# A diffusion transformer block on one core: where the attention gate's vectors are made and stored, which token tile fc1 begins with, the order of the MLP weight blocks, and TensorE's semaphore

## The chip, the cores and the metric

The kernel runs on one core of one Trainium2 chip. The metric is device time in microseconds (us) of one execution, as the median of several runs. A core has a matrix engine (TensorE, PE in the profile; PEld is its weight load), VectorE (DVE), ScalarE (ACT), GpSimd (POOL) and SyncE (SP), which here only issues DMAs. The engines run their own instruction streams in order and wait for one another through semaphores.

## The reference

One block of a diffusion transformer on 2 images of 256 tokens of width 1152, two heads of 576, an MLP of 4608. A conditioning vector per image gives six modulation vectors of 1152: shift, scale and gate for attention and for the MLP.

```python
mod = (_silu(c) @ w_mod).reshape(B, 6, 1, D)
shift_a, scale_a, gate_a, shift_m, scale_m, gate_m = [mod[:, i] for i in range(6)]
h = _layernorm(x) * (1 + scale_a) + shift_a
q, k, v = split(h @ wqkv)
attn = _softmax(einsum('bqhd,bkhd->bhqk', q, k) * Dh ** -0.5)
a = einsum('bhqk,bkhd->bqhd', attn, v) @ wo
x = x + gate_a * a
h2 = _layernorm(x) * (1 + scale_m) + shift_m
m = _gelu(h2 @ w_fc1) @ w_fc2
return x + gate_m * m
```

## The kernel before, in words

**The planner.** The kernel is written as a list of units (an operation, or a group of matmuls) on five engines. `schedule` plays the list through with costs and puts each engine's units in an order; TensorE's and SP's orders are those of the program text, the others' follow priority, and `S.in_order` fixes chosen sequences by hand. `emit` then writes the instructions, with a wait wherever one reads or overwrites what another engine made. Each instruction that is no DMA raises its engine's semaphore by one; a DMA raises one of 66 semaphores by 16 when it has landed.

**The memory.** All tiles are views of one SBUF arena, so a region serves several things in turn. Four slots hold blocks of fc1's weight, `WFC1[q % 4]`: block q, 1152 KB, has the columns of hidden tiles f = 4q to 4q+3. `WFC2` lies where `WMODR` and `WGM` (parts of the modulation weight) and, at its end, the normalized rows `XN2` lay before; it is loaded in four blocks of 2592 KB, `wfc2_load(0)` to `(3)`.

**Up to the attention.** Layer norm, the scale and shift of attention, K, then Q, the scores and softmax per image b and head h (`s_and_softmax`, index 2b+h), V (`v_proj`), then P times V (`pv`), and between its heads the matmuls of the MLP's shift and scale rows (`rows`). The softmax result is turned on VectorE (`PT_turn`) and moved by four DMAs on SP's queue.

**The attention gate** (`attn_gate`, L1059). gate_a for both images is made on VectorE, hidden under the matmuls: for each of 9 slices of the weight, kt, and each image, 1152 columns are multiplied by the image's scalar and accumulated (L1064, L1067; 18 operations). Then per image a transpose and a sum (L1073, L1075), three small copies, three adds, a cast and a transpose for both images at once (L1079 to L1085). `gate_store` puts the result into scratch memory in HBM by two DMAs, and a load per image spreads it over all 128 partitions (`GA[b]`). All four of these DMAs are on SP's queue, ahead of `wfc1_load(0)` and `(1)`.

**The output projection** (`wo_tile(t)`, t = 0 to 3, 128 tokens each; tiles 0 and 1 are image 0). Three pieces of 384 columns of 9 matmuls each; VectorE multiplies a piece by the gate as it takes it from PSUM (L1171), GpSimd adds x (L1172), VectorE makes the statistics (L751, L752, L754), GpSimd the reciprocal root (L755) and the bias (L1176, L1177), ScalarE the normalized rows `xn2_t` (L1178). Tile 1 is transposed on TensorE (`xn2_T(1)`, L1189) and modulated from PSUM (L1194 on VectorE for kt 0 to 3, L1197 on ScalarE for the rest). Tiles 0, 2 and 3 are turned on VectorE (`xn2_turn`, h2turn, L1204), moved by four DMAs each on SP's queue (`xn2_move`, L1209) and modulated in place (L1214 ScalarE, L1217 VectorE).

**fc1** (`fc1_tile(f, tok0, ntok)`): 9 matmuls into one PSUM bank, one gelu on ScalarE (L1227). The bank comes from a list `acc` that the output projection and fc2 use too. Before: f = 0 to 2 in pieces of 128 tokens, tile 0 first, then tile 1; f = 3 to 13 for image 0; f = 0 to 13 (below `F0`) for image 1, then f = 14 to 35 for all 512 tokens. The MLP's gate (`mlp_gate`, from `WGM`) is made on VectorE meanwhile; its stores and loads are on GpSimd's queue.

**fc2**: 12 output pieces of 36 matmuls in the order of j = 0 to 35, so the first block of `WFC2` (`wfc2_load(0)`), loaded last, is read first. VectorE multiplies by the gate (L1315), adds x (L1316), SP stores.

Every DMA is issued in one helper (L684), every matmul in one (L703), every transpose on TensorE in another (L706), most copies from PSUM in L698 (ScalarE) and L700 (VectorE).

Of the kernel before, what the change touches and what calls it, by code (L numbers as in the profile page):

```python
# [171 lines left out]
class Sched:  # L172
# [233 lines left out]
    def emit(self, nc, block, sems, dma_sems):  # L406
# [6 lines left out]
        dj = 0  # L413
        for e in ENGINES:
            for u in order[e]:
                for ins in u.instrs:
                    if u.dma_bytes > 0:
                        if e == "sp":
                            k = di % n_sp
                            di += 1  # L420
                        else:
                            k = n_sp + dj % n_other
                            dj += 1
                        dma_cnt[k] += 16
                        ins.dma_sem = k
                        ins.dma_val = dma_cnt[k]
                    else:
                        eidx[e] += 1
                        ins.eidx = eidx[e]
# [13 lines left out]
        for u in allu:  # L443
            e = u.eng
            kn = known[e]
            for ins in u.instrs:
                need = {}
                for d in ins.deps:
                    k, v = sem_of(d)
# [52 lines left out]
ALU = mybir.AluOpType  # L502
# [14 lines left out]
F0 = 14  # L517
# [34 lines left out]
def build_kernel(nc, x, c, wqkv, wo, w_mod, w_fc1, w_fc2, out):  # L552
# [5 lines left out]
    with (  # L558
# [75 lines left out]
        GBA = sb(O_R + FG * 17, 192)[0:32, :]  # L634
        GTA = sb(O_R + FG * 17 + 192, 192)[0:32, :]
# [423 lines left out]
        def attn_gate():  # L1059
# [10 lines left out]
            pool(100, lambda e: e.memset(GBA, 0.0), [], [GBA], "gba0")  # L1070
            for b in range(2):
                a_, t_ = ACCA[:, b, :], ACTA[:, b, :]
                dve(150 + FG * 1.1, lambda e, a_=a_, t_=t_: e.transpose(t_, a_), [a_], [t_], "ga_T%d" % b)  # L1073
                t3, o = t_.rearrange("p (g r) -> p g r", r=32), GPA[:, 0, b, :]
                dve(150 + FG * 1.1, lambda e, t3=t3, o=o: e.tensor_reduce(out=o, in_=t3, axis=AX.X, op=ALU.add), [t3], [o], "ga_red%d" % b)  # L1075
            gp = GPA.rearrange("p q b g -> p q (b g)")
            for q in range(1, 4):
                i_, o_ = gp[32 * q:32 * q + 32, 0, :], gp[0:32, q, :]
                dve(200, lambda e, i_=i_, o_=o_: e.tensor_copy(o_, i_), [i_], [o_], "ga_mv%d" % q)  # L1079
            for a_, b_ in ((0, 1), (2, 3), (0, 2)):  # L1080
                x_, y_ = gp[0:32, a_, :], gp[0:32, b_, :]
                dve(200, lambda e, x_=x_, y_=y_: e.tensor_tensor(out=x_, in0=x_, in1=y_, op=ALU.add), [x_, y_], [x_], "ga_add%d" % b_)
            g0, gb = gp[0:32, 0, :], GBA[:, 0:8 * NG]
            dve(200, lambda e: e.tensor_copy(gb, g0), [g0], [gb], "ga_bf")
            last_red[0] = dve(200, lambda e: e.transpose(GTA, GBA), [GBA], [GTA], "ga_t")  # L1085

        def gate_store():
            lin = scratch[0].rearrange("b (g c) -> (b g) c", c=32)
            dma(lin[0:64].rearrange("(j p) c -> p j c", j=2), GTA[:, 0:64].rearrange("p (j c) -> p j c", j=2), 4096, "st_ga0")
            dma(lin[64:72], GTA[0:8, 64:96], 512, "st_ga1")  # L1090

# [59 lines left out]
        acc = [3, 4, 5, 2]  # L1151
# [123 lines left out]
        wo_tile(3, {2: lambda: xn2_T(1)})  # L1275
# [26 lines left out]
        for t in range(4):  # L1302
# [4 lines left out]
            for (c0, c1) in pieces:  # L1307
# [3 lines left out]
                for j in range(JT):  # L1311
# [8 lines left out]
        ga = ["ga_%d_%d" % (b, kt) for kt in range(KT) for b in range(2)]  # L1320
        S.in_order("dve", ga)
        S.in_order("dve", ga[9:10] + ["smax_0", "snb_0"] + ga[10:11] + ["sri_0"] + ga[11:12] + ["smax_2", "snb_2", "PT_turn0", "smax_1", "snb_1", "sri_2"]
                   + ga[12:13] + ["smax_3", "snb_3", "sri_1", "PT_turn2"] + ga[13:14] + ["PT_turn1", "sri_3"] + ga[14:15] + ["PT_turn3"] + ga[15:16])
        S.in_order("act", ["sexp_0_0", "sexp_0_1", "qk_ev8", "spn_0_0", "spn_0_1", "v_ev0_0", "sexp_2_0", "sexp_2_1", "sexp_1_0", "sexp_1_1", "v_ev0_1",
                           "spn_2_0", "spn_2_1", "spn_1_0", "spn_1_1", "v_ev0_2", "sexp_3_0", "sexp_3_1", "v_ev1_0", "spn_3_0", "spn_3_1", "v_ev1_1", "v_ev1_2"])
        S.in_order("dve", ["ga_t", "mt_0", "mt_1", "OT_ev0_7", "OT_ev1_7"])
# [4 lines left out]
                           "bn_ln2_1_0", "wo_t1_1_2", "bn_ln2_1_1", "h2turn_0", "wo_t1_2_0", "bn_ln2_1_2", "aggr_ln2_1", "veps_ln2_1", "wo_t1_2_1", "bn_ln2_2_0", "wo_t1_2_2", "bn_ln2_2_1", "wo_t1_3_0", "bn_ln2_2_2", "aggr_ln2_2", "veps_ln2_2", "h2T_0_0", "h2T_0_3", "h2T_0_6", "wo_t1_3_1",  # L1331
                           "h2T_1_0", "h2T_1_1", "h2T_1_2", "h2T_1_3", "bn_ln2_3_0", "wo_t1_3_2", "bn_ln2_3_1", "h2turn_2", "bn_ln2_3_2", "aggr_ln2_3", "veps_ln2_3"])
        S.in_order("act", ["xn2_0", "xn2_1", "h2T_0_1", "h2T_0_2", "h2T_0_4", "h2T_0_5", "h2T_0_7", "h2T_0_8", "h2T_1_4", "h2T_1_5", "h2T_1_6", "h2T_1_7", "h2T_1_8", "gelu_0_0", "xn2_2"])
# [53 lines left out]
```

## Time and profile before

| | us |
|---|---|
| median of 3 runs | 242.55 (242.41 to 242.78) |
| the profiled execution | 244.14 |
| its span, first to last instruction | 242.4 |
| TensorE busy in the span | 235.8 (97%) |
| VectorE / ScalarE / GpSimd busy | 121.4 / 73.2 / 20.5 |
| mean granted TensorE clock | 0.993 of full |

A row of the timeline has the start in us, the duration in us (of a merged group: to its last end), the engine, the line, the operation, output and input, the count, and in brackets the engine's idle time before it with what ended it. In the chain of waits each piece is a start, a duration and what ran. A row of a wait names the work that came last by the profile's record. In the views of DMAs the last number is the time from issue to landing. Matmuls overlap in their pipeline and their ends are modelled, so that a busy TensorE may still be waiting a little; the pace of the operations that follow it tells more. A row of a view by windows has the stretch and its length, the busy time and count of each engine, the granted clock, the DMA engines' busy share and GB/s.

### The profile page before, as it was taken

How to read it: one execution, taken by the hardware profiler on the slowest of the kernel's cores; microseconds unless marked ns; L12 is line 12 of the kernel's file. 1: busy time of each engine (PE TensorE's matmuls, PEld its weight loads, DVE VectorE, ACT ScalarE, POOL GpSimd, SP SyncE). 2: the span in 40 equal slices, each digit the busy share in tenths (PEclk: the TensorE clock that was granted, in tenths of full speed). 3: DMA queues.
4: the chain of work that ended last, by engine and by line, in shares of the span. 5: the costliest groups of instructions: out<-in, count | busy, mean ns of one | idle time of the engine just before them, and what ended most of it. 6: DMA issues, size and time to landing. Idle time of an engine off the chain costs nothing.

```text
span 242.4 us, 4085 instructions
## 1 busy us (share of the span) xinstructions
PE 235.8 (97%) x1728; PEld 147.6 (61%) x1728; DVE 121.4 (50%) x222; ACT 73.2 (30%) x155; POOL 20.5 (8%) x42
## 2 busy tenths in 40 slices
PE   6899999999999999999998999999999999999995
PEld 2588844456567666887883444444656665665664
DVE  2644469979994598742199997000022222111112
ACT  4922440447635425875332322222000000000000
POOL 1300000000000278310000001200000000000000
PEclk9979999999999999999999999999999999999999
DMA  6999999999590875927999999991000000000000
GB/s 213 366 376 391 389 392 391 395 410 386 168 362 3 230 258 135 308 62 257 388 383 355 388 350 388 368 391 40 0 16 19 16 16 19 16 16 19 20 27 18
DMA packets 34428, 53.00 MB, mean 219 GB/s; under 512 B 4075, under 2 KB 19819, under 8 KB 34411
## 3 DMA queue, kind: packets, MB, share of 16 engines
q1 hardware_dynamic: 34016, 52.14, 61.8%
q0 software_dynamic: 224, 0.59, 0.7%
q8 instruction: 13, 0.21, 0.4%
q10 hardware_dynamic: 171, 0.01, 0.0%
q14 instruction: 4, 0.03, 0.0%
HBM read 50.15 MB, written 1.19 MB: 212 GB/s over the span
## 4 chain that ended last, share of the span: by engine, by line
PE 90%; DVE 3%; DMA 3%; POOL 1%; SPq 1%; issue 1%; ACT 0%; DVEq 0%
PE psum L703 89%; DMA arena<-in_w_mod_dram 3%; DVE arena L1171 1%; SPq L684 1%; DVE arena L751 1%; POOL arena L1172 1%; PE psum L706 0%; DVE arena L1194 0%; DVE arena L1217 0%; ACT arena L1227 0%; POOL arena L755 0%; DVE arena L1315 0%; DVE arena L752 0%; DVE arena L1316 0%; POOL arena L1176 0%
## 5 line engine op out<-in xcount | busy, mean ns | idle before, releaser
L703 PE MATMUL psum<-arena 128*128 128x384 bf16 (+8 forms) x1682 | 233.9, 308 | 3.6 <-POOL arena L729 1.5
L703 PEld LDWEIGHTS psum<-arena 128*128 128x128 bf16 (+1 forms) x1682 | 144.7, 97 | 90.6 <-issue 3.3
L1315 DVE TENSOR_TENSOR arena<-psum,arena 128x384 f32<-128x384 f32 (+2 forms) x13 | 6.9, 528 | 76.1 <-PE psum L703 76.1
L1227 ACT ACTIVATE arena<-psum 128x256 bf16<-128x256 f32 (+2 forms) x53 | 24.0, 460 | 42.2 <-PE psum L703 42.1
L698 ACT ACTIVATE arena<-psum 128x512 bf16<-128x512 f32 (+5 forms) x35 | 18.6, 561 | 31.0 <-PE psum L703 31.0
L1067 DVE SCALAR_TENSOR_TENSOR arena<-arena 128x1152 f32<-128x1152 bf16 x16 | 22.1, 1406 | 0.0
L1100 DVE SCALAR_TENSOR_TENSOR arena<-arena 128x1152 f32<-128x1152 bf16 x16 | 21.3, 1410 | 0.0
L1172 POOL TENSOR_TENSOR arena<-arena 128x384 f32<-128x384 f32 x12 | 10.9, 912 | 71.1 <-DVE arena L1171 71.0
L751 DVE BATCH_NORM_STATS2 arena<-arena 128x6 f32<-128x384 f32 (+1 forms) x18 | 9.7, 551 | 5.6 <-DMA arena<-in_x_dram 4.4
L1178 ACT ACTIVATE arena<-arena 128x1152 bf16<-128x1152 f32 x4 | 5.4, 1348 | 10.2 <-POOL arena L1177 10.2
L1171 DVE TENSOR_TENSOR arena<-psum,arena 128x384 f32<-128x384 f32 x12 | 6.5, 547 | 2.5 <-PE psum L703 2.4
L700 DVE CAST arena<-psum 128x512 bf16<-128x512 f32 x8 | 5.4, 690 | 3.5 <-PE psum L703 3.4
L1316 DVE TENSOR_TENSOR arena<-arena 128x384 bf16<-128x384 f32 (+2 forms) x13 | 6.9, 527 | 0.5
L1204 DVE STREAM_TRANSPOSE arena<-arena 128x1152 bf16<-128x1152 bf16 x3 | 4.1, 1379 | 3.6 <-ACT arena L1178 3.6
L1214 ACT ACTIVATE arena<-arena 128x128 bf16<-128x128 bf16 x12 | 5.0, 482 | 1.0 <-DMA arena<-arena 0.9
L1097 DVE TENSOR_SCALAR arena<-arena 128x1152 f32<-128x1152 bf16 x2 | 1.5, 816 | 7.5 <-DMA arena<-in_w_mod_dram 7.5
L684 POOL DMA_DIRECT2D dit_scratch<-arena x2 | 1.4, 677 | 46.2 <-DVE arena L1115 46.2
L1217 DVE TENSOR_SCALAR arena<-arena 128x128 bf16<-128x128 bf16 x15 | 3.6, 310 | 3.0 <-DMA arena<-arena 3.0
L1018 ACT ACTIVATE arena<-psum,arena 128x256 bf16<-128x256 f32 x8 | 3.7, 469 | 2.4 <-DVE arena L1015 1.9
L706 PEld LDWEIGHTS psum<-arena 128*128 128x128 bf16 (+1 forms) x46 | 3.1, 101 | 1.6 <-DMA arena<-in_c_dram 1.3
L706 PE MATMUL psum<-arena 128*128 128x128 bf16 (+1 forms) x46 | 3.6, 222 | 0.4 <-DMA arena<-in_c_dram 0.4
L755 POOL TENSOR_TENSOR arena<-arena 128x1 f32<-128x1 f32 x6 | 3.4, 564 | 4.3 <-DVE arena L754 4.1
(66 smaller groups left out, 64.6 us busy)
## 6 DMA issues: line engine op xcount, KB each, us to landing
arena<-in_w_fc_dram SPq DMA_DIRECT2D x9, 1152.0 KB, 13.7
arena<-in_w_fc_dram SPq DMA_DIRECT2D x4, 2592.0 KB, 16.8
arena<-in_wqkv_dram SPq DMA_DIRECT2D x18, 288.0 KB, 8.7
arena<-in_w_mod_dram SPq DMA_DIRECT2D x6, 864.0 KB, 12.4
arena<-in_w_mod_dram SPq DMA_DIRECT2D x3, 1728.0 KB, 21.1
arena<-in_wqkv_dram SPq DMA_DIRECT2D x1, 2592.0 KB, 17.9
arena<-in_wo_dram SPq DMA_DIRECT2D x1, 2592.0 KB, 9.6
arena<-in_w_mod_dram SPq DMA_DIRECT2D x1, 2592.0 KB, 10.6
```

The costliest lines, as they stand in the source:

```text
L698: act(c_act(n), lambda e: e.activation(out=dst, in_=src, func=ACTF.Copy), [src], [dst], name)
L700: return dve(c_dve_psum16(n) if psum16 else c_dve_psum32(n), lambda e: e.tensor_copy(dst, src), [src], [dst], name)
L703: S.instr(lambda e: e.matmul(o, lhsT=l, rhs=r, start=st, stop=sp, **kw), reads=[l, r], writes=[o])
L706: S.instr(lambda e: e.transpose(o, i_, idn), reads=[i_, idn], writes=[o])
L751: dve(550, lambda e, s=s, o=o: e.bn_stats(out=o, in_=s), [s], [o], "bn_%s_%d" % (tag, ci))
L1067: ga_units[(b, kt)] = dve(150 + FG * 1.1, lambda e, o=o, w=w, s1=s1: e.scalar_tensor_tensor(out=o, in0=w, scalar=s1, in1=o, op0=ALU.mult, ...
L1100: u = dve(1300, lambda e, o=o, w=w, s1=s1: e.scalar_tensor_tensor(out=o, in0=w, scalar=s1, in1=o, op0=ALU.mult, op1=ALU.add), [w, s1, o], ...
L1171: dve(550, lambda e, o=o, ga=ga, x1c=x1c: e.tensor_tensor(out=x1c, in0=o, in1=ga, op=ALU.mult), [o, ga], [x1c], "wo_t1_%d_%d" % (t, ci))
L1172: S.op("pool", 930, lambda e, xs=xs, x1c=x1c: e.tensor_tensor(out=x1c, in0=x1c, in1=xs, op=ALU.add), reads=[x1c, xs], writes=[x1c], name=" ...
L1227: act(c_act(ntok), lambda e: e.activation(out=dst, in_=o, func=ACTF.Gelu_apprx_tanh), [o], [dst], "gelu_%d_%d" % (f, tok0))
L1315: dve(c_dve_psum32(w), lambda e, o=o, gm=gm, t1=t1: e.tensor_tensor(out=t1, in0=o, in1=gm, op=ALU.mult), [o, gm], [t1], "fc2_t1_%d_%d" % ( ...
L1316: dve(c_dve_32(w), lambda e, t1=t1, x1c=x1c, ost=ost: e.tensor_tensor(out=ost, in0=t1, in1=x1c, op=ALU.add), [t1, x1c], [ost], "fc2_out_%d ...
```

## The change

Five things change together.

1. The attention gate is finished per image. Image 0's accumulations run first (all nine slices, with six of image 1's in front), then its transpose, sum and small operations between softmax steps, then image 1's. Image 0's two stores and its load, and image 1's two stores, go on GpSimd's queue; image 1's load stays on SP's, behind `wfc1_load(0)` and `(1)`.
2. fc1 begins with tile 1: f = 0 to 4 for tokens 128 to 255, then for 0 to 127, then f = 5 to 14 for image 0, f = 0 to 14 for image 1, the rest for all tokens (`F0` is 15). `xn2_T(1)` stands one piece of the output projection earlier, and the hand-made orders of VectorE and ScalarE put tile 1's statistics and pieces ahead of tile 0's turn and pieces.
3. The list of PSUM banks is six long from the output projection on; it was four, and six from image 1's half of fc1 on.
4. `wfc2_load(1)` no longer stands ahead of fc1's blocks 4 and 5: the order on SP's queue after `WGM` is fc1 4, 5, fc2 1, fc1 6, fc2 2, fc1 7, fc2 3, fc1 8, fc2 0. It was fc2 1, fc1 4, 5, fc2 2, fc1 6, 7, fc2 3, fc1 8, fc2 0.
5. TensorE's instructions raise its semaphore only where another engine waits for that instruction.

```diff
@@ emit @@
+        told = {d.gidx for ins in self.instrs for d in ins.deps if d.unit.eng == "pe" and ins.unit.eng != "pe"}
...
                 for ins in u.instrs:
+                    if e == "pe" and ins.gidx not in told:
+                        ins.eidx = None
+                        continue
...
-                    else:
+                    elif ins.eidx is not None:
                         bi.then_inc(sems[e], 1)
@@ build_kernel @@
-F0 = 14
+F0 = 15
...
-        GBA = sb(O_R + FG * 17, 192)[0:32, :]
-        GTA = sb(O_R + FG * 17 + 192, 192)[0:32, :]
+        GBA = [sb(O_R + FG * 17 + b * 256, 128)[0:32, :] for b in range(2)]
+        GTA = [sb(O_R + FG * 17 + b * 256 + 128, 128)[0:32, :] for b in range(2)]
@@ attn_gate @@
             for b in range(2):
-                a_, t_ = ACCA[:, b, :], ACTA[:, b, :]
+                a_, t_, gp = ACCA[:, b, :], ACTA[:, b, :], GPA[:, :, b, :]
                 dve(... e.transpose(t_, a_) ..., "ga_T%d" % b)
                 dve(... e.tensor_reduce(out=o, in_=t3, ...) ..., "ga_red%d" % b)
+                for q in range(1, 4):
+                    dve(200, ... e.tensor_copy(o_, i_) ..., "ga_mv%d_%d" % (b, q))
+                for m_, n_ in ((0, 1), (2, 3), (0, 2)):
+                    dve(200, ... e.tensor_tensor(...) ..., "ga_add%d_%d" % (b, n_))
+                pool(100, ... e.memset(gall, 0.0) ..., "gba0_%d" % b)
+                dve(200, ... e.tensor_copy(gb, g0) ..., "ga_bf%d" % b)
+                last_red[0] = dve(200, ... e.transpose(gt, gall) ..., "ga_t%d" % b)
...
+        def gate_store(b):
+            lin = scratch[0, b].rearrange("(g c) -> g c", c=32)
+            dma(lin[0:32], GTA[b][:, 0:32], 2048, "st_ga%d_0" % b, eng="pool")
+            dma(lin[32:36], GTA[b][0:4, 32:64], 256, "st_ga%d_1" % b, eng="pool")
+        def gate_load(b, eng="sp"):
+            dma(GA[b], scratch[0, b].partition_broadcast(P), P * D * 2, "ld_g%d" % b, eng=eng, run=2304)
...
-        acc = [3, 4, 5, 2]
+        acc = [2, 3, 4, 6, 5, 7]
...
-        gate_store()
-        for b in range(2):
-            dma(GA[b], scratch[0, b].partition_broadcast(P), P * D * 2, "ld_g%d" % b, run=2304)
+        gate_store(0)
+        gate_load(0, "pool")
         wfc1_load(0)
         wfc1_load(1)
+        gate_store(1)
+        gate_load(1)
...
-        wo_tile(3, {2: lambda: xn2_T(1)})
+        wo_tile(3, {1: lambda: xn2_T(1)})
...
-        for tok0 in (0, 128):
-            for f in range(0, 3):
+        for tok0 in (128, 0):
+            for f in range(0, 5):
                 fc1_tile(f, tok0, 128)
-        for f in range(3, F0):
+        for f in range(5, F0):
             fc1_tile(f, 0, 256)
-        wfc2_load(1)
         mlp_gate(last_h2T[0])
-        k = acc_rr[0] % 4
-        acc[:] = [6, 7] + acc[k:] + acc[:k]
-        acc_rr[0] = 0
...
             if f % 4 == 0 and f // 4 >= 4:
-                if f in (24, 32):
-                    wfc2_load((f - 8) // 8)
+                if f >= 24:
+                    wfc2_load(f // 4 - 5)
                 wfc1_load(f // 4)
@@ orders by hand @@
-        S.in_order("dve", ["ga_t", "mt_0", "mt_1", "OT_ev0_7", "OT_ev1_7"])
+        ... ["OT_ev0_7", "mt_0", "mt_1", "OT_ev1_7"] behind "ga_t1"
 VectorE:
-  "bn_ln2_1_1", "h2turn_0", "wo_t1_2_0", "bn_ln2_1_2", "aggr_ln2_1", "veps_ln2_1", "wo_t1_2_1"
+  "bn_ln2_1_1", "wo_t1_2_0", "bn_ln2_1_2", "aggr_ln2_1", "veps_ln2_1", "h2turn_0", "wo_t1_2_1"
...
-  "h2T_0_0", "h2T_0_3", "h2T_0_6", "wo_t1_3_1", "h2T_1_0" ... "h2T_1_3", "bn_ln2_3_0", "wo_t1_3_2", "bn_ln2_3_1", "h2turn_2", "bn_ln2_3_2"
+  "h2T_1_0" ... "h2T_1_3", ..., "wo_t1_3_1", "wo_t1_3_2", "h2T_0_0", "h2T_0_3", "h2T_0_6", "bn_ln2_3_0", "bn_ln2_3_1", "bn_ln2_3_2", ..., "h2turn_2", "h2turn_3"
 ScalarE:
-  "xn2_1", "h2T_0_1" ... "h2T_0_8", "h2T_1_4" ... "h2T_1_8", "gelu_0_0", "xn2_2"
+  "xn2_1", "h2T_1_4" ... "h2T_1_8", "h2T_0_1" ... "h2T_0_8", "gelu_0_128", "xn2_2"
```

More of the change, by code (lines that the diff above doesn't have):

```diff
@@ L413, in emit @@
         dj = 0
+        told = {d.gidx for ins in self.instrs for d in ins.deps if d.unit.eng == "pe" and ins.unit.eng != "pe"}
+        self.told = told
         for e in ENGINES:
@@ L448, in emit @@
                 for d in ins.deps:
+                    if e == "pe" and d.unit.eng == "pe":
+                        continue
                     k, v = sem_of(d)
@@ L1069, in attn_gate @@
                                                 [w, s1, o], [o], "ga_%d_%d" % (b, kt))
[L1070 removed]
             for b in range(2):
[L1072 removed]
+                a_, t_, gp = ACCA[:, b, :], ACTA[:, b, :], GPA[:, :, b, :]
                 dve(150 + FG * 1.1, lambda e, a_=a_, t_=t_: e.transpose(t_, a_), [a_], [t_], "ga_T%d" % b)
[L1074 removed]
+                t3, o = t_.rearrange("p (g r) -> p g r", r=32), gp[:, 0, :]
@@ L1075, in attn_gate @@
                 dve(150 + FG * 1.1, lambda e, t3=t3, o=o: e.tensor_reduce(out=o, in_=t3, axis=AX.X, op=ALU.add), [t3], [o], "ga_red%d" % b)
[L1076 to L1090, printed above, removed]
+                for q in range(1, 4):
+                    i_, o_ = gp[32 * q:32 * q + 32, 0, :], gp[0:32, q, :]
+                    dve(200, lambda e, i_=i_, o_=o_: e.tensor_copy(o_, i_), [i_], [o_], "ga_mv%d_%d" % (b, q))
@@ new lines, in attn_gate @@
+                for m_, n_ in ((0, 1), (2, 3), (0, 2)):
+                    x_, y_ = gp[0:32, m_, :], gp[0:32, n_, :]
+                    dve(200, lambda e, x_=x_, y_=y_: e.tensor_tensor(out=x_, in0=x_, in1=y_, op=ALU.add), [x_, y_], [x_], "ga_add%d_%d" % (b, n_))
+                g0, gall, gb, gt = gp[0:32, 0, :], GBA[b], GBA[b][:, 0:4 * NG], GTA[b]
+                pool(100, lambda e, gall=gall: e.memset(gall, 0.0), [], [gall], "gba0_%d" % b)
+                dve(200, lambda e, gb=gb, g0=g0: e.tensor_copy(gb, g0), [g0], [gb], "ga_bf%d" % b)
@@ new lines, in attn_gate @@
+                last_red[0] = dve(200, lambda e, gt=gt, gall=gall: e.transpose(gt, gall), [gall], [gt], "ga_t%d" % b)
+        def gate_store(b):
[4 more added lines that the diff above has]
+            dma(GA[b], scratch[0, b].partition_broadcast(P), P * D * 2, "ld_g%d" % b, eng=eng, run=2304)
```

16 lines of the change are left out of this document (9 added, 7 removed).

## The prediction

> **What bounds the kernel now.** I read first the page's busy shares and its chain of waits, then that chain in order of time, then ScalarE's timeline, because one gelu follows each fc1 tile and so tells TensorE's true pace.
>
> ```profile
> span 242.4 us, 4085 instructions
> PE 235.8 (97%) x1728; PEld 147.6 (61%) x1728; DVE 121.4 (50%) x222; ACT 73.2 (30%) x155; POOL 20.5 (8%) x42
> ...
> 10.38 0.74 PE psum L703 x17
> ...
> 18.35 70.08 PE psum L703 x582
> ...
> 98.91 0.47 DVE arena L1171
> ...
> 99.42 30.52 PE psum L703 x270
> ...
> 129.97 0.61 ACT arena L1227
> ...
> 130.63 109.31 PE psum L703 x648
> ```
>
> From 18.35 us on the chain is TensorE but for one stretch before 99.42 and a point at 130. So the kernel is bound by matmuls, and from there on an edit can give only what TensorE waits, or a different price per matmul. How much does it wait?
>
> ```profile
> 99.42 30.02 PEld L703 LDWEIGHTS psum<-arena 128*128 128x128 bf16 x270 [0.39 <-DVE arena L1171]
> ...
> 110.97 0.38 ACT L1227 ACTIVATE arena<-psum 128x256 bf16<-128x256 f32 x1 [0.60 <-PE psum L703]
> ...
> 113.31 0.38 ACT L1227 ACTIVATE arena<-psum 128x256 bf16<-128x256 f32 x1 [0.40 <-PE psum L703]
> ...
> 116.26 0.38 ACT L1227 ACTIVATE arena<-psum 128x256 bf16<-128x256 f32 x1 [0.60 <-PE psum L703]
> ...
> 126.09 0.38 ACT L1227 ACTIVATE arena<-psum 128x256 bf16<-128x256 f32 x1 [0.60 <-PE psum L703]
> ...
> 129.97 0.60 ACT L1227 ACTIVATE arena<-psum 128x512 bf16<-128x512 f32 x1 [1.35 <-PE psum L703]
> 132.77 0.60 ACT L1227 ACTIVATE arena<-psum 128x512 bf16<-128x512 f32 x1 [2.21 <-PE psum L703]
> ...
> 169.68 0.60 ACT L1227 ACTIVATE arena<-psum 128x512 bf16<-128x512 f32 x1 [1.35 <-PE psum L703]
> ```
>
> Undisturbed paces: ten 256-token tiles take 126.09 - 116.26 = 9.83, so 0.983 a tile or 109.2 ns a matmul (nine per tile); nineteen 512-token tiles take 169.68 - 132.77 = 36.91, so 1.943 or 215.8 ns. The two give 0.416 ns per column and 2.6 ns per matmul. Against these paces three stops stand out:
>
> Stop 1, at 99.42: 0.39, the fourth fc1 tile wants the PSUM bank that the last output projection tile's eviction (L1171, 98.91 in the chain) frees. Stop 2, image 1's first tile: 113.31 - 110.97 = 2.34 for two tiles of 0.983, so 0.37. Stop 3, tile f=16: 132.77 - 129.97 = 2.80 instead of 1.943, so 0.86. Together 1.62 us. That is nearly all that can be won in the last 224 us without faster matmuls.
>
> Stop 2 waits for the moved rows of token tile 3; stop 3 is put down to a gelu, but that gelu frees nothing the tile needs; its weight block is the likelier cause:
>
> ```profile
> 111.40 1.43 DVE L1217 TENSOR_SCALAR arena<-arena 128x128 bf16<-128x128 bf16 x6 [2.97 <-DMA arena<-arena]
> ...
> 109.68 0.59 SPq L684 DMA_DIRECT2D arena<-in_w_mod_dram  x1
> ...
> 116.25 0.42 SPq L684 DMA_DIRECT2D arena<-in_w_fc_dram  x1
> ...
> arena<-in_w_fc_dram SPq DMA_DIRECT2D x1, 1152.0 KB, 14.2
> arena<-in_w_mod_dram SPq DMA_DIRECT2D x1, 2592.0 KB, 10.6
> ...
> DMA to landing us min/median/max: 13.7/16.3/21.1
> ...
> 140.00:165.00 25.00, 25.00 (x118) 11.32 (x117) 9.88 (x13) 7.76 (x13) 2.47 (x4) 1.00 1.04 363
> ```
>
> wfc1_4 is issued at 116.25 (the moment slot 0's last reader ends) and lands 14.2 later, at 130.45; TensorE resumes at 130.63. It lay behind WGM and the 2592 KB of wfc2_1. At 363 GB/s those 2592 KB cost 7.3 us, a block of 1152 KB 3.2.
>
> **Part by part.** *fc1's blocks first.* wfc2_1 goes behind wfc1_5, so wfc1_4 no longer waits for 7.3 us of it. WGM lands at 109.68 + 10.6 = 120.3 now and about 1 us earlier then (its place behind tile 3's moves, below); 3.2 later, near 122.5, wfc1_4 has landed. It is needed at 129.1 (112.4 for image 1's first tile, below, + 15 x 0.983 + 1.943): stop 3 goes, **-0.86**. What is late next is the last load, wfc2_0, whose rows the first fc2 matmul reads. It was issued at 144.7 at the latest and landed at most 21.1 later, 165.8. Its bytes in front stay the same, and WGM, still in transfer when wfc1_4 is issued, leaves the queue no gap, so I keep 164 to 166. fc2 begins at 175.53 - 5.85 = 169.7 now (rows below), 168.1 then: 2 to 4 us spare. If this cover is gone, each late us costs one.
>
> *Six PSUM banks from the output projection on, and fc1 on tile 1.* The list [2,3,4,6,5,7] puts the last projection tile's bank behind five fc1 tiles of 128 tokens, each 9 x (128 x 0.416 + 2.6) = 0.50. The eviction then has 2.5 us: stop 1 goes, **-0.39**. The order changes what must be ready when:
>
> ```profile
> 88.45 0.56 DVE L1171 TENSOR_TENSOR arena<-psum,arena 128x384 f32<-128x384 f32 x1 [0.44 <-PE psum L703]
> ...
> 89.53 1.38 DVE L1204 STREAM_TRANSPOSE arena<-arena 128x1152 bf16<-128x1152 bf16 x1
> 90.83 0.52 DVE L1171 TENSOR_TENSOR arena<-psum,arena 128x384 f32<-128x384 f32 x1
> ...
> 93.37 1.35 ACT L1178 ACTIVATE arena<-arena 128x1152 bf16<-128x1152 f32 x1 [3.87 <-POOL arena L1177]
> 95.21 2.42 ACT L1214 ACTIVATE arena<-arena 128x128 bf16<-128x128 bf16 x6 [0.49 <-DMA arena<-arena]
> ...
> 95.57 0.67 PE L706 MATMUL psum<-arena 128*128 128x128 bf16 x9
> ...
> 175.53 0.56 DVE L1315 TENSOR_TENSOR arena<-psum,arena 128x384 f32<-128x384 f32 x1 [25.35 <-PE psum L703]
> 181.38 0.56 DVE L1315 TENSOR_TENSOR arena<-psum,arena 128x384 f32<-128x384 f32 x1 [4.70 <-PE psum L703]
> ```
>
> An fc2 tile of 36 matmuls takes 181.38 - 175.53 = 5.85, so 9 of that width take 1.46. The nine transposes of tile 1 move up by one such tile, from 95.57 to 94.11, while xn2_1 ends at 94.72 now. But h2turn_0 (1.38 at 89.53) goes behind tile 1's statistics. The eviction that waited for it (90.83) has its data one pace after 88.45, at 89.91, so it and what follows come 0.92 earlier: xn2_1 from 92.45 to 93.80. Spare 0.3 us, the tightest place; without it the price is up to 0.61, what is lacking now.
>
> Tile 0 pays: h2turn_0 starts near 91.3, 1.75 later, and its moved rows, there at 95.21 now, at about 96.96. ScalarE does tile 1's five pieces first, then tile 0's six in 2.42, to 99.4. The projection ends as before (transposes 0.50 from 95.57, then 1.46: 97.53), five tiles of tile 1 last until 100.04, so tile 0 has 0.6 spare. For tile 3, the statistics no longer queue behind h2turn_2, so I place its moved rows 1 us or more before 111.40, while TensorE comes to image 1 at 97.53 + 10 x 0.50 + 10 x 0.983 = 112.4: stop 2 goes, **-0.37**. Lost cover would give it back.
>
> *F0 = 15, halves for f 0 to 4.* f=3 and 4 (image 0) become two pieces each and f=14 two of 256: 18 + 9 more matmuls at 2.6 ns each, **+0.07**, on the path.
>
> *The gate by image.*
>
> ```profile
> 62.07 1.39 DVE L1067 SCALAR_TENSOR_TENSOR arena<-arena 128x1152 f32<-128x1152 bf16 x1
> ...
> 67.96 2.63 DVE L1073 STREAM_TRANSPOSE arena<-arena 128x1152 f32<-128x1152 f32 x2
> ...
> 73.12 0.62 DVE L1079 COPY arena<-arena 32x72 f32<-32x72 f32 x3
> ...
> 74.65 0.27 DVE L1085 STREAM_TRANSPOSE arena<-arena 32x96 bf16<-32x96 bf16 x1
> ...
> 82.34 1.02 DVE L1171 TENSOR_TENSOR arena<-psum,arena 128x384 f32<-128x384 f32 x2 [1.97 <-PE psum L703]
> ...
> 150.49 1.35 POOL L684 DMA_DIRECT2D dit_scratch<-arena  x2 [46.18 <-DVE arena L1115]
> ...
> arena<-dit_scratch SPq DMA_DIRECT2D x2, 288.0 KB, 4.6
> arena<-dit_scratch POOLq DMA_DIRECT2D x2, 288.0 KB, 7.6
> ...
> dit_scratch<-arena POOLq DMA_DIRECT2D x1, 4.0 KB, 5.8
> ```
>
> The eight small operations (73.12 to 74.92, 1.8 us) run twice, on 36 columns: 0 to 1.8 more VectorE time; I take 1.6, near the row. Image 0's transpose and sum (2.63 for the two transposes) take the slots of two accumulations, its small ones that of a third (62.07): its gate stands near 63.8, image 1's at 74.92 + 1.6 = 76.5. The first projection tile's eviction is possible five paces before 88.45, at 81.1, so the tile begins near 79.5; VectorE's casts of the attention output ahead of it have some 3 us. Hidden, cost nothing.
>
> On POOL's queue two stores are issued in 1.35 and land after 5.8, then the load after 7.6: 63.8 + 1.4 + 5.8 + 7.6 = 78.6 against 81.1 (the eviction runs at 82.34 now). POOL has no other work until then. SP, free of this wait, issues wfc1_0 and wfc1_1 behind the softmax moves, earlier than now; its next wait is for image 1's stores, 76.5 + 1.4 + 5.8 = 83.7, the load lands 4.6 later, 88.3, for an eviction at 89.9. Behind it in SP's queue stand tile 0's moves, ready at 92.7. No gain, no cost. What it costs if the cover is gone is the last rival.
>
> *TensorE's semaphore.* 1728 increments shrink to those waited on. Their price stands in no row. The 2.6 ns per matmul bound it: 1728 x 2.6 = 4.5 us if all of it were the increment, 0 if none. A loss is excluded, as nothing waits for those dropped. I take 0, since one constant fits 256, 512 and 384 columns (5850 / 36 = 162.5 = 384 x 0.416 + 2.7): a fixed charge of a matmul. The smallest matmuls on the chain are 17 of two columns (10.38): 0.74, at most 44 ns each.
> The Trainium skill, "TensorE: Matmul & The Clock Gate", section "The cost: per-tile semaphore tail", has increments of packed matmuls serialize at 26.3 ns each. If that held for these 17, an estimate of 17 x 26.3 = 0.45 us would fall from the head and the sum would be 240.55. Its section "Wait — 56ns, not 53.3ns?" gives about 2.5 ns per matmul as a fixed cost downstream of decode, which agrees with the rows and leaves 241.0.
>
> *Sum*: -0.39 - 0.37 - 0.86 + 0.07 = **-1.55** on a profiled span of 242.4, to 240.85. The profiled execution took 244.14 in all, 1.74 outside the span, which no edit touches; the median of the runs is 242.55, so 241.0.
>
> **Rivals.** *A stop that stays* (tile 1's transposes, tile 0, or bank and gelu order): half of 1.55 is left, with 0.3 and 0.6 us spare for, the earlier h2turn_0 against; 242.55 - 0.8 = 241.75. *Stop 3 is not the weight block*, but the gelu that the profile names: then 0.86 stays, 241.85; 130.45 against 130.63 speaks against it. *The increment has a price*: 241.0 - 4.5 = 236.5; the constant 2.6 is for it as much as against.
> *The GpSimd path comes late*, the slower side: xn2_1 hangs on GA[0]. Between 82.34 and xn2_1's end at 94.72 lie 12.4, now 11.5; so from a GA[0] after 94.1 - 11.5 = 82.6 on, TensorE loses us for us, and from 82.6 + 1.55 = 84.2 the kernel is slower. My 78.6 would have to be 5.6 late. If descriptors were written only once VectorE falls idle, at 76.5, the load would land at 76.5 + 1.4 + 5.8 + 7.6 = 91.3, a loss of 8.7: 242.55 - 1.55 + 8.7 = 249.7. Against it: single accumulations of 1.39 leave POOL turns between them.
> The Trainium skill, "SBUF — State Buffer", section "SBUF: two separate sides", warns of just this: VectorE in a two-port mode keeps GpSimd from writing descriptors, and it advises the SP or ACT queue. The trace of before has POOL transfers only with VectorE idle, so no run here shows it yet.
>
> **How the numbers follow.** All three stops gone 0.62; a stop that stays 0.17; stop 3 not the block 0.06; increment 0.06; late GpSimd path or late last load 0.09. The likeliest gives 241.0. Range 240.2 (0.8 of the increment's bound is real) to 242.3 (1.3 of the stops stay). 0.2% is 0.5 us, about what a measurement here can tell from no change: faster is below 242.05, which holds the first, third and fourth cases and most of the second: 0.83; same 0.08; slower 0.09.
>
> **What would show it.** After 97.5 no stop of TensorE before fc2; gelus at an unbroken pace of 1.943 over f=16; wfc1_4 landed near 123; GA[0]'s load landed before 81; xn2_1 done before the transposes; fc2's first matmul near 168.1 with wfc2_0 landed. The pace of a 384 column matmul, 162.5 ns, unchanged; if it is below, the increment had a price. Wrong: a first projection eviction after 82.6, or TensorE idle at 94.1 or 168.1.

## The result, and the profile after

The changed kernel took 241.32 us, the median of 16 runs (240.91 to 242.51), against 242.55 us of the kernel before, also 16 runs (242.10 to 242.78). The ratio is 0.9952, 95% interval 0.9943 to 0.9961, that is 0.95 to 1.38 us less. The forecast was 241.0 in a range of 240.2 to 242.3. Ratios here and below leave disturbed executions out.

| | before | after |
|---|---|---|
| median of the runs, us | 242.55 | 241.32 |
| profiled execution, us | 244.14 | 241.46 |
| its span, us | 242.4 | 239.4 |
| granted clock over the span | 0.993 | 1.000 |

The two profiled spans differ by 3.0 us and the medians by 1.23, so the spans must not be read as the gain. One stretch near the start makes most of that difference, the stretch from 10 to 15 us, where the TensorE clock granted (the number behind the engines) was 0.66 before and 1.00 after. The first row is of the kernel before, the second of the changed one; behind the window stand busy time and instruction count of TensorE, its weight loads, VectorE, ScalarE and GpSimd, then clock, DMA share and GB/s:

```profile
10.00:15.00 5.00, 4.44 (x43) 3.32 (x41) 3.76 (x14) 2.79 (x4) 0.60 (x2) 0.66 1.05 391
```

```profile
10.00:15.00 5.00, 4.25 (x55) 3.57 (x52) 3.50 (x14) 2.66 (x4) 0.67 (x2) 1.00 1.05 383
```

(1.00 - 0.66) x 5 = 1.7 us. A few executions of either kernel have a mean clock of 0.993 or 0.992 and take 1.2 to 1.7 us longer; the two others of them with a profile (the variants "fc1's weight blocks first" and "no GpSimd transfer" below) show 0.66 in the same window. The chain of waits starts its long stretch of matmuls at 18.35 before and at 16.87 after, 1.48 earlier; later positions in the two profiles are compared with that taken off.

The chain of waits of the changed kernel, in order of time (start, us, what):

```profile
span 239.4 us, 4153 instructions
PE 233.7 (98%) x1752; PEld 147.9 (62%) x1755; DVE 124.3 (52%) x230; ACT 73.4 (31%) x158; POOL 23.5 (10%) x48
...
16.87 13.60 PE psum L710 x178
...
92.79 0.50 PE psum L713 x9
93.29 143.61 PE psum L710 x990
```

The last 143.61 us are one run of matmuls: no eviction, no gelu, no weight block stands between 93.29 and 236.90, where the kernel before had three stops. The chain alone can hide a small one (that of the kernel before runs over stop 2), but ScalarE's timeline, which showed stops 2 and 3, agrees:

```profile
111.10 0.38 ACT L1236 ACTIVATE arena<-psum 128x256 bf16<-128x256 f32 x1 [0.33 <-PE psum L710]
...
125.84 0.38 ACT L1236 ACTIVATE arena<-psum 128x256 bf16<-128x256 f32 x1 [0.60 <-PE psum L710]
127.78 0.60 ACT L1236 ACTIVATE arena<-psum 128x512 bf16<-128x512 f32 x1 [1.56 <-PE psum L710]
129.73 0.60 ACT L1236 ACTIVATE arena<-psum 128x512 bf16<-128x512 f32 x1 [1.35 <-PE psum L710]
```

From 93.29 to 111.10 there is room for no stop either: two projection pieces of 1.46, ten fc1 tiles of 0.50 and ten of 0.983 end at 111.04. From 111.10 to 125.84 lie fifteen paces of 0.983, and from there the gelus follow at 1.94 and 1.95, the undisturbed paces. From 90 us on the profile names no wait of TensorE any more. What is left of the time is matmuls, the head, and what lies outside the span. That last part grew: 241.46 - 239.4 = 2.06 us after, 1.74 before. Over all 16 runs of the changed kernel time less span has a median of 2.0 (1.93 to 2.12), over the runs of the kernel before 1.73 (1.68 to 1.80).

### The profile page after: what moved, and what is told of

Its sections match the earlier page's. It is cut to its first block, busy times and chain, and to the rows that moved or that the text cites. A ratio compares the mean times of both kernels' runs of the same rounds, so it can differ in the third digit from the quotient of the medians.

```text
span 239.4 us, 4153 instructions
## 1 busy us (share of the span) xinstructions
PE 233.7 (98%) x1752; PEld 147.9 (62%) x1755; DVE 124.3 (52%) x230; ACT 73.4 (31%) x158; POOL 23.5 (10%) x48
## 4 chain that ended last, share of the span: by engine, by line
PE 94%; DMA 3%; SPq 1%; issue 0%; DVE 0%
PE psum L710 93%; DMA arena<-in_wqkv_dram 3%; SPq L691 1%; PE psum L713 1%; DVE arena L1321 0%; DVE arena L1322 0%
## 5 line engine op out<-in xcount | busy, mean ns | idle before, releaser
L710 PE MATMUL psum<-arena 128*128 128x384 bf16 (+8 forms) x1706 | 231.5, 304 | 2.9 <-POOL arena L736 1.5
L691 POOL DMA_DIRECT2D dit_scratch<-arena x6 | 3.5, 583 | 100.1 <-DVE arena L1091 53.4
L1181 POOL TENSOR_TENSOR arena<-arena 128x384 f32<-128x384 f32 x12 | 10.9, 912 | 6.4 <-DVE arena L1180 6.3
L1226 DVE TENSOR_SCALAR arena<-arena 128x128 bf16<-128x128 bf16 x15 | 4.7, 380 | 3.4 <-DMA arena<-arena 3.4
```

The source lines that it names most:

```text
L691: return S.op(eng, 500.0 if eng == "sp" else 150.0, lambda e: e.dma_start(dst, src), reads=[src], writes=[dst], name=name, dma_bytes=nbyte ...
L710: S.instr(lambda e: e.matmul(o, lhsT=l, rhs=r, start=st, stop=sp, **kw), reads=[l, r], writes=[o])
L1181: S.op("pool", 930, lambda e, xs=xs, x1c=x1c: e.tensor_tensor(out=x1c, in0=x1c, in1=xs, op=ALU.add), reads=[x1c, xs], writes=[x1c], name=" ...
```

## The experiments

Two chips were used in the first eight runs and a third for the last four; each time is compared with runs of the kernel before on the same chip (medians 242.80, 242.74 and 242.89).

**The kernel before, and the changed kernel, once more.** No edit.

> The kernel before, unchanged, to learn its span without the half clock that its profiled execution had between 10 and 15 us (0.66 granted there). Theory A (the stops of 0.39, 0.37 and 0.86 are there in every execution): 242.55, ratio 1.000, a span near 240.8 when the head runs at full clock, and the three stops together 1.5 to 1.7. Theory B (the dip made a part of the stops, which is why 1.23 was won and not 1.55): the stops sum to 1.2 to 1.3 in an execution without a dip. Theory C (the change added about 0.3 us outside the span): stops 1.6 and time minus span near 1.75, against 2.06 in the changed kernel.

> The changed kernel, unchanged, beside the next two on one chip. Time minus span was 1.73 in 29 executions of the kernel before and 2.02 in the changed one; 241.3 again, a span of 239.3.

Measured: before 242.74 (ratio 1.0005, 0.9986 to 1.0025), after 241.36 (0.9944, 0.9919 to 0.9968). In executions at a granted clock of 0.999 or more the span is 241.0 before (27 executions on the first chip; 241.0 on the two others too) and 239.4 after (11 of these 12): 1.6 us, which is what the stops come to, and more than the 1.38 that the medians of time differ by. The repeat of the kernel before shows the three stops again, with 0.38, 0.37 and 1.10 us, the third larger than in the profile that the forecast used; its clock is 1.00 from 10 to 15 us. So the stops are no part of the dip (theory B is out), and the 0.26 us outside the span, not smaller stops, are what the medians lack (theory C). Its chain of waits:

```profile
114.08 14.49 DMA arena<-in_w_fc_dram
...
128.71 109.31 PE psum L703 x648
```

and its ScalarE timeline:

```profile
127.80 0.60 ACT L1227 ACTIVATE arena<-psum 128x512 bf16<-128x512 f32 x1 [1.35 <-PE psum L703]
130.84 0.60 ACT L1227 ACTIVATE arena<-psum 128x512 bf16<-128x512 f32 x1 [2.45 <-PE psum L703]
```

130.84 - 127.80 - 1.943 = 1.10 us for stop 3, and here the chain itself names the weight block: issued at 114.08, landed 14.49 later.

**fc1's weight blocks first, alone.** The kernel before with this part only:

```
-        wfc2_load(1)
         mlp_gate(last_h2T[0])
...
-                if f in (24, 32):
-                    wfc2_load((f - 8) // 8)
+                if f >= 24:
+                    wfc2_load(f // 4 - 5)
```

> The kernel before with only the order of the weight blocks changed. Theory A (stop 3 is the late block of fc1): faster by 0.86, 241.7, gelus at 1.943 over f=16. Rival (the gelu that the profile names): 242.55, the stop of 0.86 unchanged.

**The opposite:** the changed kernel with these lines as they were.

> The changed kernel, with fc2's second weight block put back on SP's queue ahead of fc1's fourth and fifth blocks. Theory: the last block of fc1 lands after 128 us again, TensorE stops at fc1's 17th tile of features for 0.8 to 1.1 us, and the time is 242.1 to 242.4. Rival: with image 0 begun earlier the queue is ahead and the block comes in time; no stop, 241.3.

Measured: alone 241.77 (0.9959, 0.9940 to 0.9977), which is 1.03 below the kernel before on its chip, and its gelus over f=16 follow at 1.94 (129.55 and 131.49), so the rival is out; taken out of the changed kernel 242.42 (0.9975, 0.9946 to 1.0003). By the spans at a clock of 0.999 or more, the order of loads is worth 241.0 - 239.95 = 1.05 when added and 240.3 - 239.4 = 0.9 when taken out: the same from both sides. The chain of waits of the kernel with the loads put back:

```profile
114.75 13.09 DMA arena<-in_w_fc_dram
...
127.97 4.04 PE psum L710 x18
```

and two of its gelus:

```profile
127.50 0.60 ACT L1236 ACTIVATE arena<-psum 128x512 bf16<-128x512 f32 x1 [1.56 <-PE psum L710]
130.11 0.60 ACT L1236 ACTIVATE arena<-psum 128x512 bf16<-128x512 f32 x1 [2.01 <-PE psum L710]
```

130.11 - 127.50 - 1.943 = 0.67: the stop is back, in this execution (241.77, one of the two fastest of eight) just below the 0.8 to 1.1 expected. In the changed kernel the issue of the same block, from SP's timeline, and its time to landing, from the DMA issues of that microsecond (size, us to landing):

```profile
115.03 0.37 SPq L691 DMA_DIRECT2D arena<-in_w_fc_dram  x1
```

```profile
arena<-in_w_fc_dram SPq DMA_DIRECT2D x1, 1152.0 KB, 7.3
```

It lands at 122.3, for tile f=16, which TensorE begins near 127.8, where f=15's gelu starts. With 2592 KB ahead of it, it takes 13.1 instead of 7.3 us, and lands at 127.8, when TensorE has been ready for it since f=15's gelu, 127.50. So the gelu that the profile of before had named is not the cause.

**Six PSUM banks, alone.** The kernel before with

```
-        acc = [3, 4, 5, 2]
+        acc = [2, 3, 4, 6, 5, 7]
...
-        k = acc_rr[0] % 4
-        acc[:] = [6, 7] + acc[k:] + acc[:k]
-        acc_rr[0] = 0
```

> The kernel before with one thing of the change: six PSUM banks in turn from the projection on. Theory: the first of TensorE's three stops (0.37 us, at fc1's fourth tile) goes, and the other two stay: 242.3 to 242.4 beside 242.7. Rival: the moved rows are what holds TensorE in this stage, so the 0.37 us turn up at the next stop, which grows to 0.7: 242.7.

Measured: 242.81 (0.9974, 0.9945 to 1.0004), no difference that can be told; in executions at a clock of 0.999 or more the span is 241.1 (8) beside 241.0 (18). The chain of waits, and below it the last gelu of image 0 and the first of image 1, say where the 0.39 went:

```profile
94.70 15.37 PE psum L703 x162
...
110.10 0.02 ACT arena L1227
...
110.38 0.49 ACT arena L1214
...
110.92 1.16 PE psum L703 x8
```

```profile
110.10 0.39 ACT L1227 ACTIVATE arena<-psum 128x256 bf16<-128x256 f32 x1 [0.60 <-PE psum L703]
...
112.00 0.38 ACT L1227 ACTIVATE arena<-psum 128x256 bf16<-128x256 f32 x1 [0.37 <-PE psum L703]
```

Stop 1 is gone: TensorE runs unbroken from 94.70 to 110.08. There, at image 1's first tile, it stops. By the gelus, as the 0.37 of the kernel before was taken, the stop is 112.00 - 110.10 - 0.983 = 0.92: the 0.39, and a little more, has moved here. TensorE came earlier and found token tile 3's last pieces on ScalarE (L1214) still queued behind a gelu (L1227). The rival holds: the bank only moves the wait to the next late thing. The 0.39 and 0.37 of the sum are not two gains that can be had singly; in the changed kernel they go together, with the rows of tile 3 made earlier. No run isolates the start with tile 1 or the hand-made orders around tile 3; that these made the rows earlier is read from the traces (below), not shown by an experiment.

**The turn back ahead of tile 1's statistics.** The changed kernel, with VectorE's order

```
-"bn_ln2_1_1", "wo_t1_2_0", "bn_ln2_1_2", "aggr_ln2_1", "veps_ln2_1", "h2turn_0", "wo_t1_2_1"
+"bn_ln2_1_1", "h2turn_0", "wo_t1_2_0", "bn_ln2_1_2", "aggr_ln2_1", "veps_ln2_1", "wo_t1_2_1"
```

> The changed kernel, with tile 0's turn for fc1 (a VectorE instruction of 1.37 us) put back ahead of tile 1's statistics. Theory: tile 1's rows end 0.9 to 1.4 us later than 92.37, which is more than the 0.26 us that TensorE leaves between them and its transposes at 92.63; TensorE stops there for 0.6 to 1.1 us, and the time is 241.9 to 242.4. Rival: the turn's place never mattered, because the statistics wait for something else (the add of the residual on GpSimd); no stop, 241.3.

Two executions, 241.82 with the profile and 245.79 without a trace; the second has a span of 243.7 at a clock of 1.0, which nothing in the runs explains, so only the trace is read. ScalarE's and TensorE's timelines of the changed kernel at tile 1's rows and transposes:

```profile
91.02 1.35 ACT L1187 ACTIVATE arena<-arena 128x1152 bf16<-128x1152 f32 x1 [2.99 <-POOL arena L1186]
...
89.70 3.09 PE L710 MATMUL psum<-arena 128*128 128x384 bf16 x18
92.63 0.67 PE L713 MATMUL psum<-arena 128*128 128x128 bf16 x9
```

and with the turn back:

```profile
91.56 1.35 ACT L1187 ACTIVATE arena<-arena 128x1152 bf16<-128x1152 f32 x1 [3.88 <-POOL arena L1186]
...
89.83 2.60 PE L710 MATMUL psum<-arena 128*128 128x384 bf16 x15
92.96 0.68 PE L713 MATMUL psum<-arena 128*128 128x128 bf16 x9 [0.52 <-ACT arena L1187]
```

The records of neighbouring matmuls overlap by 0.16 where nothing stops (89.70 + 3.09 against 92.63), so the stop is 0.52 + 0.16 = 0.68. This execution's head was shorter: its long stretch starts at 16.51, not 16.87. So the rows came 0.54 + 0.36 = 0.90 later because of the turn, and the span grew by 0.68 - 0.36 = 0.3, to 239.7. The stop that the theory expected is there, 0.68 in 0.6 to 1.1; the time of this one execution, 241.82, is just under its 241.9 to 242.4.

**TensorE's semaphore.** Alone in the kernel before, and taken out of the changed kernel (all matmuls raise it again). The edit is the one in the diff at `told`; alone it also leaves out TensorE's waits for its own instructions.

> The kernel before with only TensorE's dropped increments. Theory A (they cost nothing): 242.55 within 0.1%, a 384-column matmul still at 162.5 ns. Rival (a price per matmul): faster by up to 4.5 us, 160 ns per matmul.

> The changed kernel with an increment on every TensorE instruction again. Theory A: 241.3, the same as the changed kernel. Rival (a price per matmul, or one outside the span): between 241.6 and 245.8.

Measured: alone 242.69 (1.0000, 0.9980 to 1.0020); taken out 241.04 (0.9927, 0.9905 to 0.9949), if anything below the changed kernel's 241.36. fc2's pace is the same with increments on all (first two rows, the changed kernel without this edit) and with the edit (last two, the changed kernel), VectorE's first two fc2 evictions 5.85 apart:

```profile
172.06 0.56 DVE L1318 TENSOR_TENSOR arena<-psum,arena 128x384 f32<-128x384 f32 x1 [24.77 <-PE psum L707]
177.91 0.56 DVE L1318 TENSOR_TENSOR arena<-psum,arena 128x384 f32<-128x384 f32 x1 [4.70 <-PE psum L707]
```

```profile
172.48 0.56 DVE L1321 TENSOR_TENSOR arena<-psum,arena 128x384 f32<-128x384 f32 x1 [24.69 <-PE psum L710]
178.33 0.56 DVE L1321 TENSOR_TENSOR arena<-psum,arena 128x384 f32<-128x384 f32 x1 [4.70 <-PE psum L710]
```

How much the edit takes out can be counted in the semaphore events of the traces: TensorE's increments fall from 1756 to 1172 in the changed kernel and from 1728 to 1144 in the kernel before, 584 fewer in both, and all of them behind 128 us. Most increments stay, because by the edit's rule an instruction keeps its own wherever one of another engine depends on it. From 166 to 238 us, in fc2, 14 are left of 469, and the pace above is unchanged. The edit is worth nothing here; what it would do to matmuls shorter than those of 384 and 512 columns, it doesn't test.

**The gate.** Three variants of the changed kernel. First, the old joint gate for both images, its stores and loads on SP's queue:

> The changed kernel with the attention gate as it was (both images at once, all on SP's queue ahead of fc1's blocks); the rest of the change stays. Theory A (the gate edit hides nothing TensorE would wait for: image 0's gate lands at 79.6 in the second execution of before, tile 1's transposes come at about 92, so it is needed by 80.5): span 239.3 and time minus span 1.73, 241.0. Rival (with the transposes one piece earlier the gate must come earlier): TensorE stops at tile 1's transposes, by 1 us, 242.0.

Second, the gate by image, but image 0's and image 1's transfers on SP's queue:

```
-            dma(lin[0:32], GTA[b][:, 0:32], 2048, "st_ga%d_0" % b, eng="pool")
+            dma(lin[0:32], GTA[b][:, 0:32], 2048, "st_ga%d_0" % b)
...
-        gate_load(0, "pool")
+        gate_load(0)
```

> The changed kernel with the gate's four stores and both loads on SP's queue, nothing on GpSimd's. Theory A (the five more transfers from GpSimd cost 0.3 us outside the span): time minus span back to 1.73, span unchanged at 239.3, so 241.0. Rival (more instructions cost it): time minus span 2.02, 241.3. Rival in the span: SP's wait holds fc1's first blocks or image 0's gate back and TensorE stops: over 241.5.

Third, no transfer on GpSimd's queue at all, the MLP gate's too on SP's queue, behind the last weight block (`wfc1_load(1)` stands behind image 1's gate there):

> The changed kernel with no transfer on GpSimd's queue at all: the attention gate's and the MLP gate's stores and loads go over SP's queue. Theory (each GpSimd transfer adds some 0.05 us outside the span): the time less the span falls from 2.0 to 1.5 us or less, with a span of 239.1 the median is 240.5 to 240.7. Rival (only the step from few to more of them counts, or it is something else): time less span stays at 1.73, median 240.9. Were the MLP gate late behind the weights, fc2's first evictions would wait for it and TensorE would stop after 173.

| | median (runs) | ratio to before | time less span | GpSimd packets |
|---|---|---|---|---|
| changed kernel | 241.36 (12) | 0.9944 (0.9919 to 0.9968) | 1.99 | 432 |
| old joint gate | 241.19 (6) | 0.9926 (0.9898 to 0.9954) | 1.73 | 224 |
| gate by image, SP's queue | 240.91 (6) | 0.9920 (0.9890 to 0.9950) | 1.74 | 224 |
| no GpSimd transfer | 241.01 (7) | 0.9910 (0.9875 to 0.9945) | 1.73 | 0 |

The packets are from the table of DMA queues, whose row for GpSimd's queue (packets, MB, share) reads in the kernel before and in the changed one:

```profile
q0 software_dynamic: 224, 0.59, 0.7%
```

```profile
q0 software_dynamic: 432, 0.89, 1.0%
```

TensorE has no stop at tile 1's transposes or behind them in any of the three (the chain's last stretch is 143.61 us in each, as in the changed kernel), so the gate by image hides nothing that TensorE waited for. What its transfers on GpSimd's queue do is add 0.26 us outside the span. All kernels with 432 packets show 2.0 there (the semaphore and the load variants as well), all with 224 or none 1.73. That the last variant is not lower than 1.73 refutes the theory of so much for each transfer: something between 224 and 432 packets (four and nine transfers) costs 0.26, and what it is stays open.

**The gate made late.** The changed kernel with one line that holds image 0's first store back until image 1's two are out:

```
+        S.in_order("pool", ["st_ga1_0", "st_ga1_1", "st_ga0_0"])
```

> The changed kernel with image 0's first store on GpSimd's queue behind image 1's two, so that its load lands near 88 in place of 75.7. Theory A (from 81 on TensorE loses us for us, at tile 1's transposes, because their rows come 11.5 after the gate): a stop of 6 to 7.5 us there, 247.5 to 249. Rival (six PSUM banks let TensorE run ahead): a loss of at most 2 us, 243.3.

Measured: 246.93, two executions of 247.72 and 246.15 (1.0163, 1.0109 to 1.0217). VectorE's first projection eviction, ScalarE's rows of tile 1, and TensorE's last projection matmuls and transposes, from the three engines' timelines:

```profile
85.36 1.02 DVE L1180 TENSOR_TENSOR arena<-psum,arena 128x384 f32<-128x384 f32 x2 [6.21 <-DMA arena<-dit_scratch]
...
94.92 1.35 ACT L1187 ACTIVATE arena<-arena 128x1152 bf16<-128x1152 f32 x1 [2.56 <-POOL arena L1186]
...
90.72 1.79 PE L710 MATMUL psum<-arena 128*128 128x384 bf16 x10
96.33 1.14 PE L713 MATMUL psum<-arena 128*128 128x128 bf16 x9 [3.81 <-ACT arena L1187]
```

The gate landed just before 85.36, some 10 us behind the changed kernel's (below), but not near 88 as expected. The rows are done at 96.27, 10.9 after that first eviction, and TensorE stands for 3.81 + 0.16 = 3.97, not for 6 to 7.5. The nine transposes then take 1.14 instead of 0.67, for the clock is down (windows view, same columns as above):

```profile
92.00:96.00 4.00, 0.51 (x4) 0.10 (x1) 3.93 (x9) 1.44 (x2) 2.92 (x6) 0.86 0.00 0
96.00:100.00 4.00, 3.67 (x18) 2.30 (x19) 3.37 (x11) 2.63 (x8) 2.93 (x5) 0.50 0.45 100
100.00:104.00 4.00, 4.00 (x40) 2.76 (x38) 1.97 (x4) 2.32 (x7) 2.06 (x4) 0.78 1.07 363
```

From 96.33 to 100 half of 3.67 is lost, and 0.22 of the next 4.00: 1.84 + 0.88 = 2.7. Stop and clock come to 6.7; the span, 245.7, is 6.3 above the changed kernel's 239.4, with a head 0.3 shorter (the matmuls ahead of the stop end at 90.72 + 1.79 = 92.51, not 92.79). The other execution has a span of 244.1 and a mean clock of 0.993: (1 - 0.993) x 244.1 = 1.7 us lost by the clock, where the profiled one has (1 - 0.986) x 245.7 = 3.4 (0.7 of it while TensorE stood), so the clock's part differs between the two. By the trace's record of the clock it is 0.50 from 94.90, 2.39 us after the last matmul (the 0.86 of the first row), to 101.73, 5.40 us after the transposes began. The Trainium skill, "TensorE: Matmul & The Clock Gate", section "Part 1: The HAM clock gate (the "warmup" mystery)", says that TensorE falls to half rate after at least one idle window of about 3.4 us and comes back after a busy one of about that length, and that the windows run freely. The 6.83 us at half rate here are two such windows; but the fall came 2.39 us after the last matmul, so here a stop shorter than 3.4 us was enough. Behind the stops of 0.37 to 1.10 us in the other runs the clock stays at 1.00.

## Why the prediction was right

*What bounds the kernel.* Right: between the stops TensorE sets the pace, and with them gone the chain is one run of 143.61 us.

*Stop 3, -0.86.* The mechanism was right, the size too small. The load order is worth 0.9 to 1.05 by the two experiments, because the block's landing varies: the stop was 0.86 in the profile read, 1.10 in the repeat and 0.67 in the profile with the loads put back. One profiled execution carries one draw of a transfer's lateness. The landing was forecast near 122.5, 121.0 without the longer head, and came at 122.3, 1.3 late, with over 5 us to spare.

*Stops 1 and 2, -0.39 and -0.37.* Both went, but the step credited the bank list with stop 1 by itself, and alone it is worth nothing: stop 2 grew from 0.37 to 0.92. The sum stands because the same change also made tile 3's rows earlier. VectorE's last pieces of tile 3:

```profile
109.00 1.43 DVE L1226 TENSOR_SCALAR arena<-arena 128x128 bf16<-128x128 bf16 x6 [1.24 <-DMA arena<-arena]
```

109.00 against 111.40, 2.40 earlier, of which 1.48 is the head: 0.92, near the "1 us or more". They are done at 110.43, ahead of image 0's last gelu at 111.10. The span's 1.6 less the 0.9 to 1.05 of the loads leaves 0.55 to 0.7 for both stops and the added matmuls, where -0.39 - 0.37 + 0.07 = -0.69 was forecast.

*Tile 1's transposes, 0.3 spare.* Rows done at 91.02 + 1.35 = 92.37 for transposes at 92.63: 0.26. The 0.92 of the turn's move was measured as 0.90, and without it the stop is 0.68, where "up to 0.61" was forecast. *Tile 0*: no stop. Its 0.6 reckoned with ScalarE's six pieces, but VectorE's three come later in the changed kernel:

```profile
96.73 1.84 DVE L1226 TENSOR_SCALAR arena<-arena 128x128 bf16<-128x128 bf16 x3
```

The last of them ends at 98.57. TensorE comes to tile 0 at 93.29 + 2 x 1.46 + 5 x 0.50 = 98.71 and reads it with the seventh matmul, 0.33 later: some 0.5 spare.

*The gate, no gain and no cost.* Right for the span, wrong outside it. GpSimd's timeline in the changed kernel, and the load's row among its DMA issues:

```profile
62.52 1.26 POOL L691 DMA_DIRECT2D dit_scratch<-arena  x2 [47.08 <-DVE arena L1091]
69.25 0.58 POOL L691 DMA_DIRECT2D arena<-dit_scratch  x1 [5.46 <-DMA dit_scratch<-arena]
```

```profile
arena<-dit_scratch POOLq DMA_DIRECT2D x1, 288.0 KB, 6.4
```

69.25 + 6.4 = 75.65, where 78.6 was forecast, 77.1 without the longer head. VectorE was busy with accumulations at that time (first row of its timeline below, from 62.74 to 71.37), and on to 75.81 with the rest of image 1's gate. The first store still landed 6.0 after its issue, beside 5.8 for one of 4.0 KB in the kernel before with VectorE idle:

```profile
dit_scratch<-arena POOLq DMA_DIRECT2D x1, 2.0 KB, 6.0
```

```profile
62.74 8.63 DVE L1074 SCALAR_TENSOR_TENSOR arena<-arena 128x1152 f32<-128x1152 bf16 x6
...
79.66 0.56 DVE L1180 TENSOR_TENSOR arena<-psum,arena 128x384 f32<-128x384 f32 x1 [0.24 <-PE psum L710]
```

So nothing waited for VectorE to fall idle, as the slower rival had it. The load, too, landed before 75.81. Some delay isn't excluded: a store of the same size issued at 76.10, when VectorE stood idle for 1.2 us, took 4.6. The warning of the Trainium skill, "SBUF — State Buffer", section "SBUF: two separate sides", is of VectorE in a two-port mode; no trace shows in which mode these accumulations run, so this run doesn't test it. The first projection eviction now follows its matmul (0.24 behind it) instead of the gate, whose load was issued at 78.38 in the kernel before and took 3.9, for an eviction at 82.34. That is 4 us of slack gained and used by nobody: the variant with the joint gate has no stop either. The step that failed is "1.74 outside the span, which no edit touches": 0.26 us came on there; without them the median would be 241.06.

*The slower rival.* Its place and working hold: the late gate's rows came 10.9 behind the eviction (11.5 forecast), TensorE stopped at the same transposes. "Us for us" holds for the stop: the gate, at 80.8 + 4.5 = 85.3, was some 4.4 us behind the limit of 82.6 less this execution's shorter head (16.59 for 18.35), and the stop was 3.97. What the rival lacked is the clock, which added 2.7.

*The semaphore, 0.* Right for fc2, where the pace of 162.5 ns is the same with 469 increments and with 14. But the bound was worked out wrong: it took all 1728 increments as gone, and 584 go. At 2.6 ns these are worth 1.5 us at most, not 4.5, so the rival's 236.5 was out of reach. The head's 17 matmuls of two columns keep all their increments in the changed kernel, so no run shows what they would cost without. The traces hint at a price there: in the kernel before these matmuls start 27 ns apart and their increments come 34 ns apart.

*The last load.* SP's timeline in the changed kernel, and the block's row among the DMA issues:

```profile
143.63 6.52 SPq L691 DMA_DIRECT2D arena<-in_w_fc_dram  x1
```

```profile
arena<-in_w_fc_dram SPq DMA_DIRECT2D x1, 2592.0 KB, 21.1
```

It lands at 164.7, and fc2 begins at 172.48 - 5.85 = 166.6: 1.9 spare, just below the 2 to 4 forecast.

*The sum.* The span fell by 1.6 (241.0 to 239.4) where 1.55 was forecast; in the two profiles, from the start of the long stretch on, by 224.05 - 222.53 = 1.52. And time less span rose by 0.26: 1.34 in all, and 1.23 and 1.38 by the two pairs of medians. The forecast was 0.3 low for that one reason.

The best version tried is the changed kernel with the gate's transfers on SP's queue, 240.91: it keeps the span and gives back the 0.26 us outside it. Its total cannot be told from the changed kernel's by these intervals; the difference of time less span can.

## What to carry to other kernels

Stops in a row on one engine are not a sum of independent gains: ask for each what comes late next if only this one goes, and make that earlier in the same change. Order a weight queue by when each block is read, and take the size of a late transfer's stop from several executions. Count what an edit really takes out before its price is bounded or its null result is read. Compare time less span as well as spans, for a change can cost there while every engine's timeline is clean.

## What the runs showed of the hardware

The time outside the span is 1.73 us with 0 or 224 packets on GpSimd's queue and 2.0 to 2.1 with 432, in every kernel of this study. A stop of 3.97 us brought 6.83 us at half the clock, beginning 2.39 us after the last matmul; stops up to 1.10 us brought none. In fc2, 455 semaphore increments fewer leave the pace of a 384-column matmul at 162.5 ns.
